# First attention of a four-layer kernel: two half-tile steps exchanged, row transposes paced, three output products one step later

## Chip, cores, metric

One core of one Trainium2 chip. The metric is the device time of one execution in microseconds (us). "Mean clock" is the mean TensorE clock that was granted over a run, 1.0 being full speed, given to three digits.

## The reference

Four residual layers on a 2048 x 576 input in bf16, in the order attention, gated layer, attention, gated layer. Cut to what matters here:

```python
def _A_ref(x, wqkv, wo):                 # 32 heads of 18, window of 8 keys at distance 2
    ...
    off = jnp.arange(W) * dil
    idx = pos[:, None] - off[None, :]
    ...
    logits = jnp.einsum('bhsd,bhswd->bhsw', q, kg) * scale
    attn = _softmax(logits, axis=-1)
    o = jnp.einsum('bhsw,bhswd->bhsd', attn, vg)
    return ... @ wo
x = A_x
x = x + _A_ref(_layernorm(x, axis=-1), A_wqkv, A_wo)
x = x + _B_ref(_layernorm(x, axis=-1), B_w_in, B_w_sp, B_b_sp, B_w_out)
...                                      # both once more
```

## The kernel before

An attention layer runs over 19 tiles of 112 query rows, each in two halves of 16 heads: 38 *half tiles*, one a step. In each step TensorE computes the scores of the next half tile (into `L_ps`), ScalarE their exponentials (`P_sb`), TensorE the products with the values of this half tile (`O_ps`), VectorE the division (`o_t`). A step also gets *fillers*: projections of later query and key columns (`pp`), value products (`pv`) and output products (`pw`).

```python
        for s in range(NST):
            if s + 1 < NST:
                L_mm(s + 1)                       # scores of the next half tile
                EXP(s + 1)
            PV(s)                                 # products with the values, division, o_t
            for f, a in table.pop(s, []):         # fillers and loads of this step
                f(*a)
```

Work that crosses partitions goes by DMA on the sync queue: projected rows are moved from `stg` into the score layout `QK` (the *moves*; GpSimd's queue takes part of them), `o_t` is transposed into `oT` (*attention transposes*), and the normalised rows of finished tiles are transposed into `xnT` (*row transposes*). Before the loop, row transposes of the layer's input do the same. The same 16 DMA engines carry the weights of the gated layer (`win2a`, `win2b`), issued on GpSimd's queue.

```python
            order = [(d, 0) for d in range(4)] + [(d, 1) for d in range(4)] + [(4, 0), (4, 1)]
            ...
            T_(12, 13, 14, 15)                    # row transposes of the layer's input
            nvw0, nvw = 4, 9
        ...
        for i in range(NS):                       # output tile i of 128 rows
            t = -(-(i + 1) * P // QT) - 1
            s = 2 * t + (6 if li == 0 and t < 10 else 5 if t < NT - 5 else 4 if t < NT - 3 else 3)
            at(s - 5, XO, i)                      # load of the residual input, for two tiles
            at(s, WO, i, 0)                       # output products, added to that input (x_new)
            at(s + 1, WO, i, 1)
            ...
            if i < NS - 1:
                at(max(s + 4, 24 + (5 * i) // 4) if li == 0 else s + 4, LN_T, i)   # row transposes
        if li == 0:
            at(0, self.load_wo, nc.sync)
            for f in reversed(self.load_win2a(nc.gpsimd)):
                at(0, f)
```

The softmax here doesn't subtract the row's maximum and nothing guards it: scores larger than these inputs give would overflow.

## Time and profile before

| what | value |
|---|---|
| time, 3 runs | 1193.89 to 1194.4 us, median 1194.13 |
| profiled run | 1192.6 us, span 1190.8 us, mean clock 0.998 |
| TensorE busy | 1180.2 us, 99% of the span |
| first attention | up to the first `pzs` product at 136.33 us |

The page gives busy times; the view of waits gives, per instruction, who ended the idle time before it; the timeline gives single instructions with start, length and, in brackets, that idle time. The lines that carry the prediction are in it. Score groups (16 score matmuls each) are good milestones, since every step has one. One group is issued before the loop; "third score group" below means the third that the loop issues.

### The profile page before, as it was taken

Reading aid. Unit: us, or ns where it says so; the run is one execution under the profiler, and the core shown is the slowest. Engines: PE = TensorE matmul, PEld = TensorE weight load, DVE = VectorE, ACT = ScalarE, POOL = GpSimd, SP = SyncE. Lnnn points to the kernel's source line nnn. Section 1 sums busy time; section 2 is a strip of 40 time slices with the busy share of each in tenths; the row PEclk is TensorE's granted clock in tenths of the full one; section 3 lists DMA queues with packets and bytes.
Section 4 is the critical chain, followed back from the end, with each engine's and each line's share of the span. In section 5 each row is a group of like instructions: output and inputs, shape, how many; then the busy total and the mean of one; then the engine's idle time right before and its main releaser. Section 6 shows DMA issues by size and latency. Waiting matters only on the chain.

```text
span 1190.8 us, 20761 instructions
## 1 busy us (share of the span) xinstructions
PE 1180.2 (99%) x8554; PEld 620.6 (52%) x8554; DVE 547.4 (46%) x1206; ACT 376.6 (32%) x593; POOL 281.5 (24%) x383
## 2 busy tenths in 40 slices
PE   8999999999999999999999999999999999999998
PEld 5567544444444444457755775444444444444677
DVE  8688587333233233245556786753233233233311
ACT  5578677210110110202156786760110110111000
POOL 4768685000000000001153877530000000000000
PEclk9999999999999999999999999999999999999999
DMA  8989992000000000049645999900000000000332
GB/s 195 200 163 199 181 224 65 23 4 9 12 12 12 12 1 11 12 139 291 169 98 117 203 227 196 202 14 9 12 12 1 12 12 12 12 1 28 125 105 73
DMA packets 178104, 101.21 MB, mean 85 GB/s; under 512 B 134336, under 2 KB 159360, under 8 KB 178009
## 3 DMA queue, kind: packets, MB, share of 16 engines
q1 hardware_dynamic: 165144, 78.13, 30.6%
q0 software_dynamic: 6512, 16.00, 5.4%
q10 hardware_dynamic: 6352, 5.75, 1.6%
q8 instruction: 67, 1.10, 0.4%
q14 instruction: 29, 0.23, 0.1%
HBM read 42.39 MB, written 16.53 MB: 49 GB/s over the span
## 4 chain that ended last, share of the span: by engine, by line
PE 94%; DMA 3%; POOL 1%; ACT 0%; issue 0%; SPq 0%; DVE 0%; ACTq 0%; DVEq 0%
PE pg L887 42%; PE pz L869 12%; PE po L941 12%; PE pz L791 11%; PE pp L402 5%; PE pw L494 3%; PE O_ps L457 3%; PE pv L379 3%; PE L_ps L437 2%; DMA oT<-o_t 2%; PE pzs L791 1%; DMA QK<-win2a 1%; POOL QK L77 1%; DMA wqk_sb<-in_A_wqkv_dram 1%; ACT P_sb L446 0%
## 5 line engine op out<-in xcount | busy, mean ns | idle before, releaser
L887 PE MATMUL pg<-Wq,Z 128*128 128x512 bf16 x2304 | 502.8, 379 | 0.0
L887 PEld LDWEIGHTS <-Z 128*128 128x128 bf16 x2304 | 225.3, 98 | 272.0
L891 DVE TENSOR_TENSOR g_tmp<-pg,ln_xn 128x512 f32<-128x512 f32 x144 | 99.6, 692 | 429.2 <-PE pg L887 429.2
L881 ACT ACTIVATE z1T<-pz 128x1024 bf16<-128x1024 f32 x72 | 73.7, 1024 | 513.8 <-PE pz L869 513.6
L77 POOL DMA_DIRECT2D wout<-in_B_w_out_dram x4 | 4.3, 1064 | 604.6 <-PE pg L887 604.6
L941 PE MATMUL po<-wout,Z 128*128 128x288 bf16 x1152 | 141.4, 286 | 0.0
L446 ACT ACTIVATE P_sb<-L_ps 128x896 bf16<-128x896 f32 (+1 forms) x152 | 126.7, 887 | 41.2 <-PE L_ps L437 40.6
L869 PE MATMUL pz<-xnT,w 128*128 128x512 bf16 (+1 forms) x640 | 136.0, 380 | 0.0
L941 PEld LDWEIGHTS <-Z 128*128 128x128 bf16 x1152 | 112.7, 98 | 28.8
L791 PEld LDWEIGHTS <-xnT 128*128 128x128 bf16 (+1 forms) x800 | 66.2, 97 | 81.0 <-issue 23.7
L791 PE MATMUL pz<-win2a,xnT 128*128 128x512 bf16 x384 | 104.8, 380 | 0.0
L892 DVE TENSOR_TENSOR Z<-g_tmp,z1T 128x512 bf16<-128x512 f32 x144 | 99.6, 692 | 9.7
L869 PEld LDWEIGHTS <-w 128*128 128x128 bf16 (+1 forms) x640 | 51.1, 97 | 80.0 <-issue 27.1
L402 PE MATMUL pp<-xnT,wqk_sb 128*128 128x512 bf16 x360 | 83.8, 382 | 0.5 <-DMA wqk_sb<-in_A_wqkv_dram 0.5
L805 ACT ACTIVATE zp<-pz 128x1024 bf16<-128x1024 f32 x64 | 65.5, 1024 | 36.6 <-PE pz L791 32.8
L951 DVE TENSOR_TENSOR x_new<-po,xo 128x288 f32<-128x288 f32 (+1 forms) x64 | 28.8, 455 | 87.6 <-PE po L941 83.5
L791 PE MATMUL pz<-win2b,xnT 128*128 128x512 bf16 (+1 forms) x256 | 65.7, 380 | 0.0
L807 DVE CUSTOM_DVE_ANT_0 Z<-zp 128x1536 bf16<-128x1536 bf16 x32 | 56.6, 1769 | 13.1 <-ACT zp L805 13.0
L77 POOL DMA_DIRECT2D QK<-stg x81 | 50.7, 631 | 36.3 <-DVE stg L371 21.0
L379 PE MATMUL pv<-wv_sb,xnT 128*128 128x288 bf16 (+1 forms) x380 | 55.8, 285 | 0.0
L242 POOL TENSOR_SCALAR ln_xn<-x_new,ln_mv,ln_rstd 128x576 bf16<-128x576 f32 x23 | 52.8, 2294 | 2.0
L402 PEld LDWEIGHTS <-wqk_sb 128*128 128x128 bf16 x360 | 33.2, 98 | 37.2 <-DMA wqk_sb<-in_A_wqkv_dram 1.0
(114 smaller groups left out, 916.9 us busy)
## 6 DMA issues: line engine op xcount, KB each, us to landing
xres<-x_new SPq DMA_DIRECT2D x48, 288.0 KB
xo<-xres SPq DMA_DIRECT2D x32, 288.0 KB
wout<-in_B_w_out_dram POOLq DMA_DIRECT2D x4, 1296.0 KB, 8.5
xo<-xres SPq DMA_DIRECT2D x8, 576.0 KB
w<-in_B_w_in_dram SPq DMA_DIRECT2D x16, 256.0 KB
QK<-stg POOLq DMA_DIRECT2D x53, 72.0 KB, 4.4
QK<-stg SPq DMA_DIRECT2D x41, 72.0 KB
xo<-in_A_x_dram SPq DMA_DIRECT2D x8, 288.0 KB
```

The lines of the kernel that those rows point to most:

```text
L77: return eng.dma_start(out=out, in_=in_)
L379: nc.tensor.matmul(pv[:nk, 0:288], lhsT=self.xnT[:, c, QT * t:QT * t + nk], rhs=wv_sb[:, c, hh * 288:(hh + 1) * 288], start=(c == 0), stop ...
L402: nc.tensor.matmul(pp[:, :], lhsT=w, rhs=self.xnT[:, c, PADL + cc * 512:PADL + (cc + 1) * 512], start=(c == 0), stop=(c == 4))
L446: nc.scalar.activation(out=P_bufs[(2 * s + jp) % 4][:nk, :, :, 0:nq], in_=Lv[:nk, :, :, 0:nq], func=ACT.Exp, scale=scale)
L791: nc.tensor.matmul(pzvs[ci][:, sub * 512:sub * 512 + w], lhsT=self.xnT[r0:r1, c, PADL + i * P:PADL + (i + 1) * P], rhs=win2(c)[r0:r1, c0 + ...
L805: nc.scalar.activation(out=zp[:, c0:c0 + cn], in_=pzvs[ci][:, 0:cn], func=ACT.Gelu_apprx_tanh, accum_out=sums[:, ci:ci + 1])
L869: nc.tensor.matmul(pz1s[q // 2][:, q % 2, :], lhsT=w1[r0:r1, c, sub * P:(sub + 1) * P], rhs=self.xnT[r0:r1, c, PADL + q * 512:PADL + (q + ...
L881: nc.scalar.activation(out=z1T[:, q2 * 512:(q2 + 2) * 512], in_=pz1s[q2 // 2][:, :, :].rearrange("p a b -> p (a b)"), func=ACT.Gelu_apprx_ ...
L887: nc.tensor.matmul(pg[:, :], lhsT=Z[:, jj, i, sub * P:(sub + 1) * P], rhs=Wq[q][:, i, :], start=(i == 0), stop=(i == NS - 1))
L891: nc.vector.tensor_tensor(out=tmp[:], in0=pg[:, :], in1=bsp[:, qs], op=ALU.add)
L892: nc.vector.tensor_tensor(out=uT(jj)[:, sub, qs], in0=tmp[:], in1=z1Ts[jj, sub][:, qs], op=ALU.mult)
L941: nc.tensor.matmul(acc[hh], lhsT=uT(j // 2)[:, j % 2, i * P:(i + 1) * P], rhs=wouts[j // NJH][:, j % NJH, hh * 288:(hh + 1) * 288], start= ...
```

## The change

It is meant for the first attention alone: let the second half tile that is computed be one whose rows arrived early (second and third step exchanged), split a weight load, start row transposes at step 19 with about one per attention tile, and put the output products of tiles 4 to 6 one step later, so that they don't wait for attention transposes. Core of the diff, cuts marked:

```diff
-        for c0, n, w0 in ((D, 512, D + 64), (0, D, 0), (D + 512, 64, D)):
+        parts = dict(k=(D, 512, D + 64), q=(0, D, 0), q0=(0, 256, 0), q1=(256, D - 256, 256), k1=(D + 512, 64, D))
+        for c0, n, w0 in (parts[k_] for k_ in names):
...
+        seq = list(range(NST))
+        if li == 0:
+            seq[1:3] = 2, 1
...
-            self.load_wqk(nc.sync)
+            self.load_wqk(nc.sync, ("k", "q0", "q1", "k1"))
...
-                    at(13 * hh, VW, t, hh, True)
+                    if hh == 1:
+                        at(0, VW, t, hh, True)
...
-            s = 2 * t + (6 if li == 0 and t < 10 else 5 if t < NT - 5 else 4 if t < NT - 3 else 3)
+            s = 2 * t + (7 if li == 0 and 5 <= t <= 7 else 6 if li == 0 and t < 10 else 5 if t < NT - 5 else 4 if t < NT - 3 else 3)
             at(s - 5, XO, i)
             at(s, WO, i, 0)
...
-                at(max(s + 4, 24 + (5 * i) // 4) if li == 0 else s + 4, LN_T, i)
+                at(s + 4 if li > 0 or i > 12 else 19 + 2 * i if i < 8 else 35 + (i - 8) // 2, LN_T, i)
         if li == 0:
+            at(1, self.fill_window_rows, QK, 1, ((4, 0),))
+            at(2, self.fill_window_rows, QK, 1, ((4, 1),))
             at(0, self.load_wo, nc.sync)
-            for f in reversed(self.load_win2a(nc.gpsimd)):
-                at(0, f)
+            w2l = self.load_win2a(nc.gpsimd)
+            for k_ in (3, 5, 4, 2, 1, 0):
+                at(0, w2l[k_])
...
         if li == 0:
             VW(nvw - 1, 0, False)
             VW(nvw - 1, 1, False)
+            VW(nvw, 0, True)
+            self.fill_window_rows(QK, 1, ((0, 0), (0, 1)))
         for s in range(NST):
             if s + 1 < NST:
-                L_mm(s + 1)
-                EXP(s + 1)
-            PV(s)
+                L_mm(seq[s + 1])
+                EXP(seq[s + 1])
+            PV(seq[s])
```

More of the change, by code (lines that the diff above doesn't have):

```diff
@@ L185, in make_ident, with fill_window_rows @@
                                 base=0, pattern=[[-1, P]], channel_multiplier=1)
-    def fill_window_rows(self, QK, half):
+    def fill_window_rows(self, QK, half, parts=((0, 0), (0, 1), (4, 0), (4, 1))):
         nc, n = self.nc, self.cfg.S // 2
@@ L193, in fill_window_rows @@
         c0 = PADL + half * n
-        for g0 in (0, 4):
-            for a in range(2):
-                nc.vector.tensor_copy(out=QK[:, a, g0:g0 + 4, c0:c0 + n].rearrange("p g (k x) -> p g k x", x=256),
-                                      in_=self.pat[:, a, None, None, PADL:PADL + 256].to_broadcast([P, 4, n // 256, 256]))
+        for g0, a in parts:
+            nc.vector.tensor_copy(out=QK[:, a, g0:g0 + 4, c0:c0 + n].rearrange("p g (k x) -> p g k x", x=256),
+                                  in_=self.pat[:, a, None, None, PADL:PADL + 256].to_broadcast([P, 4, n // 256, 256]))
     def H_tile(self, name):
@@ L284, in zero_right, with load_wqk @@
         nc.vector.memset(R["wo"][64:128, 4, :], 0.0)
-    def load_wqk(self, eng):
+    def load_wqk(self, eng, names=("k", "q", "k1")):
         R = self.right
-        for c0, n, w0 in ((D, 512, D + 64), (0, D, 0), (D + 512, 64, D)):
+        parts = dict(k=(D, 512, D + 64), q=(0, D, 0), q0=(0, 256, 0), q1=(256, D - 256, 256), k1=(D + 512, 64, D))
+        for c0, n, w0 in (parts[k_] for k_ in names):
             self.dma(R["wqk"][:, :, w0:w0 + n], self.A_wqkv[0:512, c0:c0 + n].rearrange("(c p) n -> p c n", p=P), eng=eng)
@@ L425, in layer_A @@
         NST = 2 * NT
+        seq = list(range(NST))
+        if li == 0:
+            seq[1:3] = 2, 1
+        pbi = {s: 2 * k_ for k_, s in enumerate(seq)}
         L_tiles = {}
@@ L445, in EXP @@
                 Lv = L_ps[:, :, 0:4 * QT].rearrange("p a (b c) -> p a b c", c=QT)
-                nc.scalar.activation(out=P_bufs[(2 * s + jp) % 4][:nk, :, :, 0:nq], in_=Lv[:nk, :, :, 0:nq], func=ACT.Exp,
+                nc.scalar.activation(out=P_bufs[(pbi[s] + jp) % 4][:nk, :, :, 0:nq], in_=Lv[:nk, :, :, 0:nq], func=ACT.Exp,
                                      scale=scale)
@@ L457, in PV @@
                         nc.tensor.matmul(O_ps[:, idx * (DH + 1):(idx + 1) * (DH + 1)],
-                                         lhsT=P_bufs[(2 * s + jp) % 4][:nk, jj, ftl, :],
+                                         lhsT=P_bufs[(pbi[s] + jp) % 4][:nk, jj, ftl, :],
                                          rhs=v_ext[:nk, t, 16 * hf + idx, :], start=True, stop=True)
@@ L509, in LN_XN @@
                 k_, m = divmod(i - 4, 3)
-                xn = stgs[(2 + k_) % NSTG][:].rearrange("p a b -> p (a b)")[:, 640 * m:640 * (m + 1)]
+                xn = stgs[(1 + k_) % NSTG][:].rearrange("p a b -> p (a b)")[:, 640 * m:640 * (m + 1)]
             tails[i]["xn"] = self.ln_xn(tails[i]["x"], P, mv, rstd, nmr, eng="pool", xn=xn)
@@ L650, in layer_A @@
             for hh in range(2):
-                VW(t, hh, li == 0)
+                VW(t, hh, li == 0 and t > 5)
         pieces = []
@@ L698, in layer_A @@
             if k_ == (2 if li == 0 else 0):
-                L_mm(0)
-                EXP(0)
+                L_mm(seq[0])
+                EXP(seq[0])
             PG(d, qk, cc, li > 0 or k_ < 4, q2)
-            if li == 0 and k_ == 3:
-                self.fill_window_rows(QK, 1)
         if li == 0:
```

## The prediction

> **What bounds the kernel now.** I read the page's busy times first, then TensorE's own waits, then windows of single stages, then the timeline around each gap.
>
> ```profile
> PE 1180.2 (99%) x8554; PEld 620.6 (52%) x8554; DVE 547.4 (46%) x1206; ACT 376.6 (32%) x593; POOL 281.5 (24%) x383
> ```
>
> TensorE is busy for 1180.2 of 1190.8 us, so the most that any rescheduling can win from recorded idleness is 10.6 us, 0.9%. All its waits in the run:
>
> ```profile
> PE pw L494 <- DMA oT<-o_t: 1.8, 2, 1.2
> PE L_ps L437 <- ACT P_sb L446: 1.6, 5, 0.4
> PE warm L541 <- POOL ident L184: 1.5, 1, 1.5
> PE pt L574 <- DVE ln_xn L567: 1.2, 2, 0.8
> PE L_ps L437 <- DMA QK<-win2a: 0.7, 1, 0.7
> PE pp L402 <- DMA wqk_sb<-in_A_wqkv_dram: 0.5, 1, 0.5
> ```
>
> The change touches only the first attention (up to about 136 us); the second takes the old branches, and the gated stage between them is unbroken TensorE work in the chain of waits. So a microsecond won before 136 us reaches the end whole. Busy time hides two more losses, and the windows show them (columns: length, busy time of PE, PEld, DVE, ACT, POOL with counts, granted clock, DMA share, GB/s):
>
> ```profile
> 45.00:50.00 5.00, 4.24 (x53) 2.63 (x50) 4.67 (x6) 3.75 (x6) 5.00 (x6) 1.00 1.13 220
> 50.00:55.00 5.00, 5.00 (x76) 2.41 (x74) 2.84 (x7) 2.98 (x5) 1.05 (x2) 0.66 1.07 372
> 80.00:102.60 22.60, 21.64 (x439) 15.83 (x437) 18.15 (x57) 20.18 (x26) 21.33 (x23) 1.00 0.97 197
> 123.80:136.50 12.70, 10.88 (x148) 6.62 (x144) 9.23 (x28) 5.29 (x11) 9.29 (x10) 1.00 0.97 199
> 712.20:722.90 10.70, 10.70 (x149) 6.72 (x145) 9.09 (x28) 5.35 (x11) 9.35 (x10) 1.00 1.05 211
> ```
>
> See the clock of 0.66 just after the gap at 48 us, ScalarE's 20.18 of 22.6 us in the third line, and that the last two lines are the same work (end of first and of second attention): 12.7 us against 10.7. In the timeline:
>
> ```profile
> 48.86 0.22 PE L437 MATMUL L_ps<-QK 32*128 32x112 bf16 x1 [0.69 <-DMA QK<-win2a]
> ...
> 50.90 2.29 PE L402 MATMUL pp<-xnT,wqk_sb 128*128 128x512 bf16 x5
> ...
> 54.08 1.24 PE L402 MATMUL pp<-xnT,wqk_sb 128*128 128x512 bf16 x5
> ...
> 131.51 1.39 PE L494 MATMUL pw<-wo_sb,oT 128*128 128x288 bf16 x10 [1.23 <-DMA oT<-o_t]
> ```
>
> The first score group of step 1 (heads 16 to 31) waits for the last moves of its rows; soon after it the same five projections take 2.29 us instead of 1.24; near the end an output product waits for a transpose.
>
> **What the Trainium skill says.** (1) "TensorE: Matmul & The Clock Gate", Part 1, What's actually happening: the clock is halved after a low-activity window of 4096 cycles at 1.2 GHz, 3413 ns, free-running. The trace agrees: windows of 0.1 us show the clock at 0.50 from 50.52 to 53.93 us, 3.4 us, after the thin stretch at 47.3 to 50.5. The page speaks of an idle window; here TensorE was recorded idle for only 0.7 us of it. (2) "SBUF — State Buffer", SBUF: two separate sides (the box on the DVE-blocks-DMA trap): a VectorE copy in a two-port mode keeps GpSimd from writing DMA descriptors. The trace agrees: the last of these moves is issued at 44.65 us in 1.34 us, when VectorE's four row fills (4.64 us from 44.68) begin, while the moves just before took 0.51 to 0.57. (3) "DMA: Bandwidth & Descriptors", Issuing engines are not separate DMA queues: all share the same 16 engines. The trace agrees: at 102.6 to 123.8 us, where row transposes come nearly one a step, the DMA share is 1.19.
>
> **The change part by part.** A step is scores of the next half tile (16 matmuls, 0.33 us in the chain), products of this one (0.50), and filler: a projection (five of 218 ns, 1.09), a value or output product (0.61 to 0.63).
>
> *Query weights in two loads.* The first query projection waits at 14.47 us, 0.55 us, for a load of 648 KB (576+72); its first 256 columns are 288 KB. At the 300 GB/s and more that the windows there show, 360 KB are 1.1 us, more than the wait. The projections are unbroken up to 47 us, so 0.55 us stay won.
>
> *Exchange of the second and third step.* Step 2 is heads 0 to 15 of the next tile, whose rows came earlier. Its scores don't wait; those of step 1 come a step later. I lay it out from the start of the first scores in question: scores 0.33, products 0.50, value product 0.63 (the second half of tile 9, moved here from step 13), half of the scores of step 1 to 1.62; their other half needs the second exponential of step 2, which ends at about 2.0 (0.25 plus two of 0.87); then products 0.50 and a projection 1.09: end at 3.8. Before, 47.28 to 53.19 is 5.91, with the first half of tile 9's value product in it, which now comes ahead: 5.91 against 4.43, 1.48 us won, and 0.63 of work done in advance. The rows of step 1 land before 48.82; its scores now come at about 48.9 with everything 0.55 earlier, and the move is issued up to 0.79 us sooner, since the fills start after tile 9's value product. So they should not wait. I count the clock as whole: of the 1.48, 1.05 is the slow projection; the slow 0.74 us up to 53.93 give another 0.25.
>
> *Fills and value copies.* Two fills (1.16 us each) before the loop and one in each of steps 1 and 2, behind a projection's copy. VectorE then lags: it needs about 1.5 us a step (0.26+0.46+0.69 and gaps) against TensorE's 2.1, and with four PSUM buffers I find its releases just in time (fifth products: 57.5 against 57.8). Four value copies move to ScalarE, which was idle from 34.84 to 41.78: nothing gained or lost.
>
> *Output products of tiles 4 to 6 one step on; value product taken from step 13.* In steps with one filler ScalarE bounds: steps 14 to 17 took 80.47 to 87.85 us, 1.845 each, for 1.44 of TensorE's work. Steps 13 to 24 took 24.19 us. After: steps 13 to 17 at 1.84 less some slack, 8.9; 18 to 22 with two fillers at 2.12, 10.6; step 23 1.84; step 24 2.1: 23.4. So 0.75 us of it, most of it the value product done earlier. The aim, I read, is that these products don't wait for attention transposes that the sync queue issues late (the one ready at 79.6 us was issued at 85.41).
>
> *One row transpose per attention tile, from step 19.* Before they begin at step 24 and come nearly one a step; the queue holds the attention transpose of tile 15, ready at 119.80, until 121.02 and that of tile 16, ready at 125.31, until 126.80, which lands at 131.38. Per tile the queue then needs about 1.2+1.2+0.55+0.25 = 3.2 of 4.3 us, where two row transposes made it 4.4. The second attention runs at this pace and has no such wait: 712.25 to 722.89 is 10.64 us for what took 12.69 (123.84 to 136.53). So 2.05 at most; I count 1.7, as VectorE still delivers late.
>
> Sum: 0.55+1.48+0.25+0.75+1.7 = 4.7 us. 1194.1 less 4.7 is 1189.4.
>
> **The rivals.** *A new low-clock window:* step 16 loses its only filler, 0.83 of work in 1.84 us. Over 3.4 us around it TensorE has about 2.3 of work, 67%, against about 1.9, 55%, in the window that lost its clock. For it speaks that 55% was enough; against it that 129 to 132 us, with 1.23 us idle, kept the clock at 1.00. It would cost 1 to 1.7 us: about 1190.8. If the old drop stays too, 1192. *The early row transposes delay the attention transposes:* one issued at 90.38 landed only at 99.89 (the chain of waits), which stalled VectorE by 1.59 us at 99.99, and now two or three row transposes and second-stage weights share that stretch. Against it: the second attention has this mix and no such wait. It would eat 1 to 3 us: 1190.5 to 1192.5. *The last moves of step 19's heads:* sync issues them from 80.99 to 84.78, and their scores start at 87.85; the input load that stood before them has gone behind, 0.6 us, while steps 13 to 17 shrink less than that. A wait is possible, under 1 us. *VectorE becomes the bound of steps 1 to 5* through the fills: each tenth it lags, TensorE pays; at most 0.5. *Nothing in the loop matters:* then only 0.55 comes, 1193.5; but step 1's wait and the 131.51 one lie on TensorE itself.
>
> **Range and chances.** All gains together with the full 2.05 and a little more in the exponential-bound steps give 1187.5; two rivals at once give 1192. A gain of 2% would be 23.9 us, more than twice all idleness; a loss of 2% would need a new stall in a stage that isn't touched. So faster 1%, slower 1%, same 98%.
>
> **What would show each step.** Right: no wait for query weights at 14 us and none for moved rows at 48; a clock of 1.00 in 45 to 55 us and the first projection in the loop at 1.24; steps 13 to 17 still about 1.84 apart; no output product waiting for a transpose at the end; the end of the first attention as long as the second's, 10.6 us. Wrong: a clock of 0.50 for 3.4 us around 50 or 85; VectorE or TensorE waiting for attention transposes near 95; score groups waiting for moved rows near 87.

## The result

| kernel | runs | median us | range | mean clock of the profiled run |
|---|---|---|---|---|
| before, same rounds | 6 | 1193.18 | 1191.21 to 1194.4 | 0.998 |
| changed | 6 | 1193.52 | 1191.78 to 1197.89 | 0.994 |

The ratio is 1.001, 95% interval 0.9991 to 1.003: the same time. A ratio is the mean time of one kernel's fast runs over that of the other's of the same rounds, so not quite the ratio of the medians. The prediction said 1189.4, with a range of 1187.5 to 1192: too low.

The profile of the changed kernel fell on its slowest run (1197.89 us), so what follows from it was checked on other traces. Those of e1, e3, e4, e5, e6 and e12 are of the slowest run of their kernel too, so the traces show losses more often than the timed runs have them. Its busy time, from the page:

```profile
PE 1182.9 (99%) x8554; PEld 621.0 (52%) x8554; DVE 546.5 (46%) x1202; ACT 377.5 (32%) x597; POOL 277.0 (23%) x383
```

All waits of TensorE in it:

```profile
PE pp L402 <- issue: 3.3, 1, 3.3
PE L_ps L441 <- ACT P_sb L450: 2.5, 7, 0.4
PE pt L578 <- DVE ln_xn L571: 1.9, 3, 0.8
PE warm L545 <- POOL ident L184: 1.5, 1, 1.5
```

The waits for query weights, for moved rows at 48.9 us and for a transpose near the end are gone, as predicted. A new one of 3.3 us is there. "issue" means that the wait view found no releaser; the chain of waits that leads to this projection tells more (start, length, what):

```profile
44.79 7.79 DMA xnT<-ln_xn
52.58 1.14 issue
53.72 2.29 PE pp L402 x5
```

A row transpose of the layer's input, the third of the last four, took 7.79 us to land. The 1.14 us after it are the fourth: the semaphore on which it counts is complete at 53.63 us, 7.46 us after its issue at 46.17, and the projection's first weight load starts at 53.69. The windows (columns as in the prediction) show what came with it, and the end of the first attention in the last line:

```profile
45.00:50.00 5.00, 4.65 (x76) 3.21 (x75) 2.51 (x3) 3.77 (x7) 3.49 (x5) 1.00 1.20 166
50.00:55.00 5.00, 1.71 (x20) 0.82 (x19) 1.83 (x6) 1.14 (x2) 0.88 (x2) 0.75 1.01 271
55.00:60.00 5.00, 5.00 (x73) 2.24 (x72) 3.14 (x6) 2.05 (x3) 0.00 (x0) 0.57 0.49 172
82.30:105.96 23.66, 22.54 (x429) 15.74 (x428) 17.93 (x53) 18.66 (x24) 19.99 (x24) 0.86 0.90 195
130.10:140.80 10.70, 10.70 (x149) 6.72 (x145) 8.91 (x28) 5.20 (x11) 9.05 (x10) 1.00 0.98 196
```

The stretch from 45 to 50 us is fuller than before (4.65 against 4.24 us busy), but the clock falls twice: to a mean of 0.57 in 55 to 60 us, and to 0.86 in the long stretch. In the clock records both are 6.83 us at 0.50, from 52.5 and from 90.04 us. The end of the first attention takes 10.7 us, TensorE without a gap, as the second attention did. The timeline around the first trouble:

```profile
47.38 0.40 PE L441 MATMUL L_ps<-QK 32*128 32x112 bf16 x16
...
49.57 0.37 PE L441 MATMUL L_ps<-QK 32*128 32x112 bf16 x8 [0.35 <-ACT P_sb L450]
49.87 0.56 PE L461 MATMUL O_ps<-v_ext,P_sb 128*128 128x19 bf16 x16
53.72 2.29 PE L402 MATMUL pp<-xnT,wqk_sb 128*128 128x512 bf16 x5 [3.29 <-issue]
```

The exchanged scores start without a wait at 47.38, those of step 1 wait only for the exponentials: the exchange works as intended. Right behind it the first projection of the loop stands 3.29 us, and runs at half speed. So TensorE reaches the end of the first attention (first `pzs` product) at 140.61 us, 4.28 later than in the profile of before.

### The profile page after: what moved, and what is told of

It reads as the page before. It is cut to its first block, busy times and chain, and to the rows that moved or that the text cites. A ratio compares the mean times of both kernels' runs of the same rounds, so it can differ in the third digit from the quotient of the medians.

```text
span 1196.1 us, 20760 instructions
## 1 busy us (share of the span) xinstructions
PE 1182.9 (99%) x8554; PEld 621.0 (52%) x8554; DVE 546.5 (46%) x1202; ACT 377.5 (32%) x597; POOL 277.0 (23%) x383
## 4 chain that ended last, share of the span: by engine, by line
PE 96%; DMA 1%; DVE 1%; ACT 1%; issue 1%; POOL 0%; SPq 0%; ACTq 0%; DVEq 0%
PE pg L895 42%; PE pz L877 12%; PE po L949 12%; PE pz L799 11%; PE pp L402 7%; PE pv L379 3%; PE pw L498 3%; PE O_ps L461 3%; PE L_ps L441 2%; PE pzs L799 1%; DMA xnT<-ln_xn 1%; DMA oT<-o_t 1%; ACT P_sb L450 1%; DVE ln_st L558 0%; PE pt L479 0%
## 5 line engine op out<-in xcount | busy, mean ns | idle before, releaser
L959 DVE TENSOR_TENSOR x_new<-po,xo 128x288 f32<-128x288 f32 (+1 forms) x64 | 28.8, 456 | 87.9 <-PE po L949 83.7
```

## Experiments

All outputs are right. The times of "before" in a batch are those of the same chip and rounds. Unless an edit is marked otherwise it is against the changed kernel.

### Is the new wait in every run, and what causes it?

**e1_again**: the changed kernel, unaltered.

> The changed kernel again, unaltered, for a second profile and more times. Theory A (the changed kernel's own schedule lost the gain: the last row transpose before the loop lands late, and step 16 without filler loses the clock): the first projection of the loop waits 2 us or more for a transposed row tile again, a clock of 0.50 shows for one or two windows of 3.4 us after step 16 or after that wait, and the end of the first attention takes 10.6 to 10.7 us as in the profile after; the time is within 2 us of before. Theory B (the profiled run of 1197.89 us was an accident): no such wait, and the time is 3 to 5 us under before.

Median 1193.83 (1192.32 to 1195.75) against 1191.06, ratio 1.001 (0.9991 to 1.003). Its trace has the wait again, with its releaser named:

```profile
52.87 1.45 PE L402 MATMUL pp<-xnT,wqk_sb 128*128 128x512 bf16 x5 [2.66 <-DMA xnT<-ln_xn]
```

The clock is at 0.50 for 3.41 us from 53.77 and for 6.83 us from 87.9. Two of its six runs had a mean clock of 1.0, so the low clock is not in every run.

**e3_weights_later**: the second stage's first weight loads at step 3 instead of step 0.

```diff
-                at(0, w2l[k_])
+                at(3, w2l[k_])
```

> The changed kernel with the six loads of the second stage's weights issued at step 3 and not at step 0. Theory A1 (these loads, which the exchange brought forward, crowd the last row transpose): the transpose lands at 48 to 50 us, the first projection of the loop doesn't wait, and the time is 2.5 to 4 us under the changed kernel's. Rival A2 (the transposes are slow by themselves, or held by the semaphore eight DMAs back): the wait of 2 to 3 us stays and so does the time.

1199.13 (1197.48 to 1200.61) against 1191.06, ratio 1.0051 (1.0031 to 1.0072): slower. The wait for the row transpose is gone (the fourth lands 2.7 us after its issue), and so is the low clock near 50 us; but in its place, from the view of waits and from the chain:

```profile
PE pw L498 <- DMA oT<-o_t: 5.5, 1, 5.5
```

```profile
59.58 11.86 DMA oT<-o_t
```

The six loads were issued from 58.01 to 61.31 us, around that attention transpose, and a low clock follows, 6.83 us from 68.49. So the transfers that are late lie beside the loads at either place: row transposes at step 0, an attention transpose at step 3.

**e5_loads_behind_moves**: the same six loads at step 0 in another order: those whose place in `win2a` still serves as `stg` buffer go first, so that all six wait for it (in the trace, until the third row transpose, which reads it, has landed at 48.30 us).

```diff
-            for k_ in (3, 5, 4, 2, 1, 0):
+            for k_ in (2, 1, 0, 3, 5, 4):
```

> The changed kernel with one line altered: the six weight loads of the second stage in the order 2, 1, 0, 3, 5, 4. Piece 2 overwrites rows that are still being moved out, so it and all behind it are issued only when those moves have landed (about 47 us in the first experiment, where the loads began at 44.6). Theory A1 (early loads crowd the last row transpose): the last row transpose lands by 50.5 us, the first projection's wait of 2.7 to 3.3 us shrinks to under 0.8, and the time falls by 2 us or more against the changed kernel where no low-clock window differs. Rival A2 (transposes are slow by themselves): the wait stays.

1191.84 (1190.26 to 1194.99) against 1191.08, ratio 1.0006 (0.9992 to 1.0021). The issue of these loads in the timeline, kernel before first:

```profile
44.65 1.34 POOL L77 DMA_DIRECT2D QK<-win2a  x1 [0.57 <-DMA QK<-win2a]
45.99 5.07 POOL L77 DMA_DIRECT2D win2a<-in_B_w_in_dram  x6
```

The changed kernel:

```profile
42.55 2.09 POOL L77 DMA_DIRECT2D QK<-win2a  x4 [0.17 <-issue]
44.63 1.68 POOL L77 DMA_DIRECT2D win2a<-in_B_w_in_dram  x3
```

This run:

```profile
48.40 3.88 POOL L77 DMA_DIRECT2D win2a<-in_B_w_in_dram  x6 [4.11 <-DMA xnT<-ln_xn]
```

In this trace of before, the last move was issued while VectorE's fills ran, and took 1.34 us; the loads began at 45.99 us. The change put these fills later, so the moves went out faster, as I had predicted, and three weight loads began at 44.63 us, in the middle of the four row transposes (issued from 42.14 to 47.43 us). Begun at 48.40, they do no harm: no wait for a row transpose, no low clock near 50 us, and the third score group starts at 51.22 us (55.95 and 54.25 in the two traces of the changed kernel). The packets fit. The transposes move as packets of 256 bytes, the weights as packets of 4608. In the kernel before, about 1660 packets of 256 bytes were carried from 46 to 49 us; in the changed kernel 240 from 48 to 51 us, where the weight packets take 0.74 to 1.06 us each instead of 0.2 to 0.3. Why they take longer there isn't shown; VectorE's last two fills run at that time (47.86 to 50.22 us).

Five traces have the changed order of loads and all four transposes. In each the first projection starts within 0.15 us of the fourth transpose's landing, also where the view puts the wait to VectorE (e2, e13); and its wait is long where the loads begin early: 2.66, 3.29, 1.78, 0.57 and 0.31 us for loads from 44.46, 44.63, 44.73, 44.94 and 45.12 us (e1, the changed kernel, e17, e2, e13). Nor is the old order safe. In e4 and e8 below, which keep the old fills and loads, the last move went out just before the fills, in 0.51 us, the loads began at 44.32 and 44.44 us, and the first projection waits for a row transpose as well, 1.30 us (e4) and 0.39 us (e8):

```profile
51.30 1.24 PE L402 MATMUL pp<-xnT,wqk_sb 128*128 128x512 bf16 x5 [1.30 <-DMA xnT<-ln_xn]
```

So loads that begin early go with that wait in either kernel; with the change they begin early more often (five of five traces at 45.12 us or before, against two of six: before, e4, e8, e10, e14, e18).

**e6_last_row_tile_on_pe**: the last of the four row tiles is transposed by TensorE instead.

```diff
-            T_(12, 13, 14, 15)
+            T_(12, 13, 14)
...
+        if li == 0:
+            T_pe(15)
```

> The changed kernel with the row transpose of tile 15 done by TensorE (5 matmuls, about 0.3 us, and one copy on ScalarE) and not by a DMA: it takes away what the first projection waits for. Theory A: no wait there, the low-clock window at 50 to 57 us goes, the loop's third score group starts at about 51.6 us (54.2 and 56.0 in the two profiles of the changed kernel); time 2 to 3 us under the changed kernel's. The window at 88 us stays. If the gain shows at 56 us but not in the total, a wait for attention transposes at steps 18 to 26 has taken it.

1192.08 (1191.03 to 1193.03) against 1191.08, ratio 1.0005 (0.9992 to 1.0019). The wait is gone too, the third score group starts at 51.70 us. So two independent edits take the wait away; but that brings the time only to that of before, and the intervals of both overlap that of the changed kernel (0.9991 to 1.003): the gain is seen in the traces, not in the times.

### Low clock in the thin steps, and step (c)

**e2_products_back**: the output products of tiles 4 to 6 at their old steps.

```diff
-            s = 2 * t + (7 if li == 0 and 5 <= t <= 7 else 6 if li == 0 and t < 10 else ...)
+            s = 2 * t + (6 if li == 0 and t < 10 else ...)
```

> The changed kernel with the output products of tiles 4 to 6 back at their old steps, so that step 16 has a filler again. Theory A: no low clock near 90 us; 1.5 to 3 us faster than the changed kernel in those of its runs that lose that window, about equal in the others; a wait of the early row tile stays. Rival (the shift was needed against late attention transposes): output products at steps 16 to 20 wait for attention transposes, up to 2 us, and the time is no better.

1194.27 (1193.42 to 1195.95) against 1191.06, ratio 1.0016 (0.9997 to 1.0035). No low clock at 80 to 92 us in its trace, but 2.4 us of waits for attention transposes, the longest 1.7, and low clock at 50.52 and 108.54 us. The time is that of the changed kernel. Its trace has new waits in place of the low clock near 90 us; that these just make up for it is not shown.

**e7_and_filler_in_step16**: as e6, with five unread matmuls of 288 columns in step 16, the one that lost its only filler.

```diff
+        def FILLER():
+            pf_ = self.PT_tile([P, 512], f32, "idle_fill")
+            for _ in range(5):
+                nc.tensor.matmul(pf_[:, 0:288], lhsT=self.ident[:], rhs=wv_sb[:, 0, 0:288], start=True, stop=True)
...
+        for s_ in (16,) if li == 0 else ():
+            at(s_, FILLER)
```

> As e6, and step 16 gets five matmuls of 288 columns whose result nobody reads (0.62 us, in time in which TensorE waits for ScalarE anyway). Theory (low activity of step 16 loses the clock): no low-clock window at 85 to 97 us in the profile, and the median clock of the runs rises to 0.999 or more; another 1.5 to 3 us under e6. Rival (the attention transposes bound this stretch, and the slow clock only fills a wait that would stand there anyway): the window goes, but an output product at steps 18 to 26 then waits 1.5 to 4 us for an attention transpose and the time stays.

1192.16 (1190.27 to 1196.43) against 1191.08, ratio 1.001 (0.9992 to 1.0029). Its trace has full clock from start to end. The steps 13 to 24 nevertheless take 26.21 us (24.19 before), since VectorE waits for the residual input of an output product:

```profile
84.88 0.42 SPq L77 DMA_DIRECT2D xo<-in_A_x_dram  x1
```

```profile
89.65 0.46 DVE L501 TENSOR_TENSOR x_new<-pw,xo 128x288 f32<-128x288 f32 x1 [3.83 <-DMA xo<-in_A_x_dram]
```

That load moved with its product, to behind four moves in the sync queue: issued at 84.88 us, landed at 89.65; in the kernel before it was issued at 80.38. TensorE lost 1.5 us to it.

**e9_input_load_back**: as e7, the load at its old step.

```diff
-            at(s - 5, XO, i)
+            at(s - 6 if li == 0 and 5 <= t <= 7 else s - 5, XO, i)
```

> The kernel of the run with the last row tile on TensorE and the filler, with one more edit: the residual input loads for the output products of tiles 4 to 6 are issued at their old steps, while the products stay one step later. Theory (the load that was moved with its product lands too late): there the load was issued at 84.88 us and landed at 89.65, VectorE waited 3.8 us for it and TensorE 1.5. Issued one step earlier it stands before the moves, near 80.4 us as in the kernel before, so that wait disappears, and the time from the 14th to the 26th score group falls from 26.06 us to between 23.3 and 24.5. First pzs product then at 132 to 133.2 us (134.48 there), the whole 1.3 to 2.5 us less than that kernel's clean 1190.3, near 1188.3 (median of before about 1191). Rival (second-stage weight loads starve whatever is in flight there): the load is issued earlier but lands as late, or the wait passes to attention transposes, and the stretch stays at 26 us. Second rival: with that wait gone the steps run into the next attention transpose at about 100 us, as in the run with the row transposes alone, and 1 to 3 us come back there.

1191.09 (1190.5 to 1192.59) against 1191.41, ratio 0.9998 (0.9983 to 1.0013). The load is issued at 79.84 us, VectorE's wait is gone, and the first `pzs` product starts at 133.49 us (134.48 in e7). From the 14th to the 26th score group, the one before the loop counted, it took 24.93 us, a little over my 24.5, and the median missed my 1188.3 by 2.8 us.

**e11_load_back_no_filler**: the same without the filler.

> As the run with the input load back, but without the unread filler products in step 16. If the low clock near 86 us came from the step that lost its filler alone, one window of 3.41 us at a halved clock stays at 80 to 92 us and costs up to 1.7 us against the run with filler (1190 against 1188.3). If it came from the wait for the input load and the thin step together, the clock stays at 1.00 there and both kernels have the same time.

1191.77 (1190.37 to 1195.21) against 1191.41, ratio 1.0003 (0.9987 to 1.0019). The same stretch of both, first e11, then e9:

```profile
76.67:88.00 11.33, 10.21 (x216) 7.12 (x216) 8.23 (x25) 9.19 (x12) 10.88 (x14) 0.82 0.92 163
```

```profile
76.57:88.00 11.43, 10.56 (x228) 7.75 (x227) 8.14 (x25) 10.11 (x12) 10.98 (x14) 1.00 0.97 161
```

Without filler the clock drops (0.82, third number from the right; in the clock records 6.83 us at 0.50 from 83.96 us), with it it stays. The first `pzs` product comes at 134.62 instead of 133.49 us, although the filler's 0.61 us of work are not done: the window costs about 1.7 us against e9, and 2.4 against e16, which has fewer waits there. Over all traces: the eight of changed kernels with the thin step (the changed kernel, e1, e3, e5, e6, e11, e13, e17) all have low clock that begins between 80 and 93 us. In seven of them it begins 0.5 to 2.5 us after step 16; in e13 it begins 6.9 us after it, behind a wait of 1.32 us for VectorE, so that the thin step is an unlikely cause (e5 has another before step 16, at 80.87). Of the five with the filler, e7, e9 and e16 have none, e12 and e15 have it, after a wait of more than 1 us there. Of the six that are the kernel before or one part of the change on it, e10 and e18 have it. The timed runs are a check with more cases, though they don't tell where the clock was low: 7 of the 47 of kernels with the thin step have a mean clock of 1.0, 15 of the 28 with the filler, 34 of 71 of the kernel before; in the pair e11 and e9 it is 1 and 3 of 6. Part of this is other windows, as the one near 53 us. So the thin step is not the only cause and doesn't act in every run, but with it a low clock is much more frequent.

### Other parts by themselves

**e4_row_transposes_only**: the kernel before with the new row-transpose steps.

```diff
-                at(max(s + 4, 24 + (5 * i) // 4) if li == 0 else s + 4, LN_T, i)
+                at(s + 4 if li > 0 or i > 12 else 19 + 2 * i if i < 8 else 35 + (i - 8) // 2, LN_T, i)
```

> The kernel before with one part of the change alone: one row transpose per attention tile. By my prediction the end of the first attention shrinks from 12.7 to 10.7 us and the time falls by 1.7 to 2.1 us, with nothing else changed up to 98 us (the low-clock window at 50 us stays). Rival (early row transposes delay the attention transposes at 90 to 100 us): VectorE waits for them for 2 us or more there and half the gain or more is lost.

1191.72 (1189.61 to 1195.22) against 1191.06, ratio 0.9995 (0.9973 to 1.0017). The trace is that of its slowest run, 1195.22 us: an output product waits 3.3 us for an attention transpose before 107.63 us, and low clock follows from 107.89. A loss of that size doesn't fit its runs at 1189.61 and 1190.03. That the early row transposes delayed it is likely, as they are the edit, but one trace doesn't show it. The wait for a row transpose before the loop's first projection (above) is in this trace too.

**e8_exchange_only**: the kernel before with `seq` alone.

> The kernel before with one part of the change alone: the second and third step exchanged. By my prediction the wait of 0.69 us for moved rows and 1.4 us of the gap at 47 to 49 us go. Theory A1 (here the weight loads start no earlier than in the kernel before, about 46 us): the last row transpose lands at about 50 us, the first projection waits less than 0.8 us, so 0.5 to 1.2 us faster than before. Rival: the first projection waits for the row transpose for 2 us or more here too, because the wait of step 1 had merely hidden it, and nothing is won.

1191.78 (1191.05 to 1192.32) against 1191.08, ratio 1.0004 (0.999 to 1.0017). The second-step wait is gone, the third score group starts at 51.55 us; near the end an output product waits 2.0 us for its transpose and the clock drops from 130.26 us. Exchange and row transposes may need each other; but one trace is little for that, and together they bring no more.

**e10_query_split_only**: the kernel before with the query weights in two loads.

> The kernel before with the query weights in two loads and nothing else. My step (a) says 0.55 us are won: no wait for these weights at 14 us, first scores 0.5 to 0.6 us earlier, everything up to the gated stage 0.55 us earlier unless a later wait eats it (the row moves at 48.86 us then wait longer, since their transfers are set by VectorE and GpSimd: rival, gain 0.2 or less). It also tells whether the 0.75 us that the end of the program lost in the changed kernel comes with this part: 3.05 us from the last product to the end if not, about 3.75 if so.

1192.71 (1191.08 to 1196.26) against 1191.41, ratio 1.0011 (0.9994 to 1.0028). First scores at 40.53 us, but they come at 40.89 and 40.80 in the two later traces of before, which have no wait for these weights. So 0.3 to 0.4 us, not 0.55; and in six traces of changed kernels the time of these scores varies by 0.3 us (40.37 to 40.65). And from the last product to the end this kernel takes 3.7 us, where before takes 3.05.

### The end of the program

Each row is from one trace. The transfers of the sync queue, and ScalarE's last output with them, count on eight semaphores in turn; in the last column but one is the place, in the order in which the closing block waits for them, of the one on which the last output counts:

```
kernel               last output lands   its place   last product to end
before, e14               2.1 us           8th           3.05 us
changed                   2.1              2nd           3.80
e2                        2.1              2nd           3.42
e10 (query split)         2.4              2nd           3.7
e9                        2.1              1st           3.88
e12, e13                  2.1              1st, 2nd      3.88, 3.84
e16, e17                  2.1              8th           3.06, 3.05
```

**e12_last_piece_on_act_queue** (e9 with one small weight load issued by ScalarE's queue) and **e13_changed_end_restored** (the changed kernel with two):

```diff
-            self.load_wqk(nc.sync, ("k", "q0", "q1", "k1"))
+            self.load_wqk(nc.sync, ("k", "q0", "q1"))
+            self.load_wqk(nc.scalar, ("k1",))          # e13; e12: only its 64-row piece
```

> The kernel of the input load back (last row tile on TensorE, filler, input load at its old step), with one small weight load (64 rows of the last 64 key columns) issued by ScalarE's queue instead of the sync queue. In the trace the sync queue's transfers count on eight semaphores in turn, and the closing block waits for these one after the other, about 0.07 us each. In the kernel before, the last output lands on the eighth of them (2.13 us after the last product) and the end is at 3.05; the query weights in two loads shift the turn, the last output lands on the first or second, six or seven waits follow it, and the end is at 3.7 to 3.9. Theory: with one transfer less on the sync queue it lands on the eighth again, and last product to end is 3.0 to 3.1 us: 0.7 us won, median near 1190.4 where before has about 1191.3, the fastest runs near 1189.8. Rival (the longer end comes from fetching instructions at another place of the stream): the end stays at 3.4 us or more.

> The changed kernel with both loads of the last 64 key columns issued by ScalarE's queue, so that the sync queue has as many transfers as before. Theory: last product to end 3.0 to 3.1 us against 3.75; all else, the wait for the last row transpose near 53 us too, as in the changed kernel: 0.7 us less than it, about 1193.0, still above before. Rival as in the run before this one: the end stays at 3.4 or more.

1191.42 (1190.23 to 1194.08) and 1192.32 (1190.62 to 1195.6) against 1191.32, ratios 1.0001 (0.9988 to 1.0013) and 1.0011 (0.9997 to 1.0025). Inconclusive for the end: the last output still landed on the first or second semaphore, so the edit didn't change what it was to change. The traces gave something else: e12, with the load in front of the moves again, waits for moved rows,

```profile
PE L_ps L441 <- DMA QK<-stg: 1.5, 2, 1.1
```

and e13, with the load behind them, has VectorE waiting 3.2 us for the load. So each of two transfers can be late behind the other; but not in every run, for e9 and e16 have the load in front as well and don't wait for moved rows.

**e16_last_piece_on_gpsimd_queue** (e9) and **e17_changed_end_restored_again** (the changed kernel), with the small loads on GpSimd's queue instead:

```diff
+            self.load_wqk(nc.gpsimd, ("k1",))          # e17, after the set-up; e16: only its 64-row piece
```

> The runs that moved small loads to ScalarE's queue left the last output on the first or second semaphore of the turn, so both hardware queues share the turn and those runs didn't test the theory. Here the input-load-back kernel has the 64-row piece of the last key columns on GpSimd's queue, which counts on other semaphores. Theory: the last output lands on the eighth semaphore as in the kernel before, one wait follows it, and last product to end is 3.0 to 3.1 us instead of 3.9: 0.8 us won, a median of about 1190.3 to 1190.8 where before has 1191.3, and runs with full clock near 1189.8. This is also my candidate to beat both kernels, at most by 0.1%. Rival (another place in the instruction stream makes the end longer): it stays at 3.4 or more.

> The changed kernel with both loads of the last 64 key columns on GpSimd's queue, so that the hardware queues have as many transfers as before. Theory: last product to end 3.0 to 3.1 us against 3.75, the rest as in the changed kernel (a wait for the last row transpose near 53 us, one or two low-clock windows): median 1192.5 to 1193.2, runs with full clock near 1191.7 against 1192.4. Rival: the end stays at 3.4 or more.

1191.51 (1189.34 to 1193.27) and 1192.98 (1190.48 to 1195.56) against 1192.02, ratios 1.0001 (0.9983 to 1.0019) and 1.0011 (0.9992 to 1.003). The last output counts on the eighth semaphore, and the end is back at 3.05 us in both: the extra two transfers of the split query load had shifted the turn, and six or seven waits of about 0.07 us, one of them 0.4 in the changed kernel, e9, e12 and e13 (in e2 none, and its end is 3.42), stood behind the last output. Why one is longer is open. This explains 0.75 us of the 1197.89 us run, in e2 0.37. In the rest, e17 behaves as the changed kernel: a row transpose is waited for 1.78 us, and there are low-clock windows at 52.73 and 86.86 us.

The profiled run of e16 (1189.34 us, span 1187.6) is the cleanest of all; TensorE's waits in it:

```profile
PE L_ps L441 <- ACT P_sb L450: 2.4, 7, 0.4
PE pz L888 <- issue: 1.6, 10, 0.2
PE warm L551 <- POOL ident L184: 1.5, 1, 1.5
PE pt L585 <- DVE ln_xn L578: 0.8, 2, 0.5
```

No wait for a transfer is left (the second line stands at places where matmul records are missing: the trace has 8467 matmuls for 8564 weight loads). It is my candidate to beat both kernels, and it doesn't beat the one before: its other five runs took 1190.39 to 1193.27 us.

**e15_second_weights_every_third_step**: e12 with the later weight loads spread.

```diff
-            at(PG_END + 2 + 2 * k_, win2b_piece, k_)
+            at(PG_END + 2 + (3 if li == 0 else 2) * k_, win2b_piece, k_)
```

> As the first of these four, and the six later weight loads of the second stage begin every third step (16, 19 to 31) instead of every second (16, 18 to 26). Theory (these loads slow the attention transposes): VectorE's wait for oT transposes between 85 and 100 us (1.4 us, which TensorE paid with 0.58) goes away, and up to 0.6 us are won against that kernel; rival: the loads meet the row transposes later, at 103 to 118 us, and delay transposes there, so that nothing is won or up to 2 us lost.

1193.52 (1191.37 to 1194.4) against 1191.32, ratio 1.0015 (1.0003 to 1.0027). Slower by more than its reason can tell: 1.8 us of waits for moved rows near 86 us and 6.83 us of low clock from 87.18, before the spread loads matter. It settles nothing about these loads.

### Were the losses that I counted in every run of before?

**e14_before_again** and **e18_before_third_trace**: the kernel before, unaltered.

> The kernel before, unaltered, for a second trace. Theory: the low clock at 50.5 us that I counted as a loss of every run is in some runs only (24 of 33 runs of it had a mean clock of at least 0.999). If this trace has full clock, the first pzs product begins near 134.6 us instead of 136.33, the third score group near 51.9 instead of 53.13, and the output product near the end still waits 1 us or more for its transpose. Rival: it's there again at 50 us, and clean runs differ in something else. Ratio 1.000.

> The kernel before once more, for a third trace. Of its 55 timed runs beside my experiments 27 had a mean clock of 1.0 and a mean time of 1190.4 us, 2 us less than the run whose profile I predicted from. Theory (the losses that my steps (b) and (d) counted are not in every run): if this run has full clock, the first pzs product begins at 133 to 134.2 us (136.33 in the profile that I read, 135.02 in the second trace), the projection in step 1 takes 1.24 us, and the output product near the end waits 0.7 us or less for its transpose; the run's time is then 1189.2 to 1191. If it has a low-clock window at 50 us again, it is 1191 to 1193.5. Rival: with full clock the first attention ends at 135 to 136.3 us all the same, and the 2 us are elsewhere.

1191.76 (1189.91 to 1193.08) against 1191.32, ratio 1.0003 (0.999 to 1.0016); and 1191.94 (1190.42 to 1199.72) against 1192.25, ratio 1.0015 (0.9978 to 1.0052). The windows that showed the low clock, e14 then e18:

```profile
50.00:55.00 5.00, 5.00 (x75) 2.41 (x74) 2.81 (x7) 2.90 (x5) 0.74 (x2) 0.66 1.05 366
```

```profile
50.00:55.00 5.00, 4.89 (x89) 2.77 (x88) 3.31 (x9) 4.32 (x6) 0.84 (x3) 1.00 1.05 365
```

In e18 the clock is full there: 89 matmuls instead of 75 in the same 5 us. Its timeline:

```profile
48.15 0.22 PE L437 MATMUL L_ps<-QK 32*128 32x112 bf16 x1 [0.92 <-DMA QK<-win2a]
...
50.17 1.24 PE L402 MATMUL pp<-xnT,wqk_sb 128*128 128x512 bf16 x4
51.34 0.70 PE L437 MATMUL L_ps<-QK 32*128 32x112 bf16 x16
...
130.32 1.39 PE L494 MATMUL pw<-wo_sb,oT 128*128 128x288 bf16 x10 [1.10 <-DVE o_t L464]
```

The wait for moved rows is there in all three traces (0.69, 1.0 and 0.92 us). But the slow projections are not, and without them the kernel before reaches its third score group at 51.34 us, as early as the best changed one. e18 has its low clock at 84.16 us instead, so neither run is a trace of before with full clock throughout; such a trace I don't have.

Timed runs by their mean clock (of before, the 62 beside the experiments):

```
kernel                      runs   mean us    at clock 1.0: runs   mean us
before                       62    1191.8            29            1190.5
changed (with e1)            12    1194.0             2            1192.4
e9                            6    1191.4             3            1191.4
e16                           6    1191.4             5            1191.0
```

With the nine runs of e14 and e18, before has 71 runs, mean 1191.9, of which 34 at clock 1.0 take 1190.6. Chips differ, so the rounds matter: in those of e9 and e16 before took 1190.2 and 1189.9 us at clock 1.0 (five runs each). At full clock both candidates are thus about 1 us behind it.

## Why the prediction was wrong

Two steps failed. The exchange, 1.48 + 0.25 of the 4.7 us, was counted from a loss that not every run of before has; against a run without it, it wins nothing (-0.12 us). And the sum holds nothing for what the change itself costs: a row transpose that lands late (up to 3.29 us), a clock window in the thin step (1.7 to 2.4), and the end of the program (0.75).

**The base.** I took 4.7 us off 1194.1, the median of three runs. Of 62 later runs of the same kernel 29 had full mean clock and took 1190.5 us on average, and the mean of all is 1191.8. The three lay high (only 6 of the 62 took 1193.89 us or more), and the profiled run (1192.6) had low clock at 50 us. The losses were real, but some were of that run and not of the kernel. My own sentence "a microsecond won before 136 us reaches the end whole" holds; that each loss there is in every run was never said and silently used. The base is not what made the number too low: 4.7 us off 1191.8 would be 1187.1, further off still.

**Step by step**, the prediction's figure first; then what e16, which has all parts of the change and no accident, wins in its trace against the profile I read and against the two later traces of before. The times of both kernels stand in brackets; the five filler matmuls of e16 are taken off with 0.61 us, what they lengthen step 16 (2.05 us in e9, 1.44 in e11). The first row still holds 0.28 us for the five transposing matmuls of e6 (38.20 to 38.48 us in e16), which the change as given doesn't have: without them it reads 0.85, 0.43 and 0.34.

| step | predicted | against the first profile | against e14 | against e18 |
|---|---|---|---|---|
| query weights: start to first score group | 0.55 | 0.57 (41.31, 40.74) | 0.15 (40.89) | 0.06 (40.80) |
| exchange: group before the loop to its third | 1.48 + 0.25 | 1.16 (11.82, 10.66) | 1.84 (12.50, low clock) | -0.12 (10.54) |
| steps 13 to 24 | 0.75 | 0.32 (24.19, 23.87) | 0.09 (23.96) | 1.82 (25.69, low clock) |
| end of first attention | 1.7, at most 2.05 | 2.05 (12.69, 10.64) | 0.89 (11.53) | 1.05 (11.69) |

*Query weights and end.* The working was right for the run that I read, even to the 2.05 that I cut to 1.7. But the wait for query weights is in one of three traces of before, and near the end, where the same output product waits in all three (1.23, 0.72 and 1.10 us), the first profile has a second wait for a transpose of 0.6 us. As a difference between kernels these two steps are about 0.4 and 1.0.

*Exchange.* 1.05 of its 1.48 and the 0.25 were the low clock, which "I count as whole". e18 has full clock there, and the exchange wins nothing against it: the value product done ahead costs 0.60 us (6.58 us from the group before the loop to the loop's first, against 5.98), and from the loop's first to its third e16 takes 4.08 us for my 3.8, since the scores wait 0.35 us for exponentials. Two more traces with full clock there agree: the old order takes 10.16 us in e10, the exchange alone 10.60 in e8. That is the step of the prediction that failed most.

*Steps 13 to 24.* ScalarE's bound was right: for six steps, 13 to 18, I had 8.9 and 2.12, 11.02 us; e16 took 11.63 with the filler, and e13, without it and at full clock there, 11.21. The other six took 12.85 us for my 12.42 (four of 2.12, 1.84 and 2.1); steps 23 and 24 alone took 4.28 for my 3.94, as their scores wait 0.42 us for exponentials. So 0.3 instead of 0.75, and 0.1 against the quicker e14.

Against a run of before with no low clock I therefore estimate 0.4 - 0.1 + 0.1 + 1.0, about 1.4 us, from the entries without it.

**What took even this 1.4 us**, none of it in the sum:

1. A row transpose of the layer's input lands late (3.29, 2.66, 1.78, 0.57 and 0.31 us of TensorE's time in the traces of the changed kernel, e1, e17, e2 and e13). The prediction saw that the move would be "issued up to 0.79 us sooner", and stopped there; what stood behind the moves on GpSimd's queue, weight loads, came 1.36 us sooner than in that profile as well. e5 and e6 show it; e4 and e8 show that the old order can meet it too.
2. Low clock in the thin step. It was the first rival, with a cost of "1 to 1.7 us", and it came in seven of the eight traces with that step. I had named it and given it no place in the predicted time.
3. The residual input's load. The prediction used its later place ("has gone behind, 0.6 us") as a help to the moves and did not ask who waits for the load. e7 and e9 show it, where nothing earlier hides it. e12 and e15 have the load in front and pay at the moves, the third rival; e9 and e16 have it there and do not.
4. The end: 0.75 us through the turn of the semaphores, shown by e16 and e17. No step or rival of mine had it.

The second rival (early row transposes delay attention transposes) is seen in the one trace of e4, 3.3 us; its median shows no loss, so how often it happens is open. VectorE's lag in steps 1 to 5 was not found: in e16 those steps have no wait for it. The third point that the prediction takes from the skill is shown less well than it says: a DMA share of 1.19 shows busy engines, not that queues share them; e5 speaks to that.

With these removed one by one (e5, e6, e9, e16) the changed kernel comes back to the time of before, not below it (ratios 1.0006, 1.0005, 0.9998 and 1.0001, each within noise of the 1.001 of the changed kernel); of what is left of its gain 0.61 us go into the filler and 0.28 into the transposing matmuls. e16's runs at clock 1.0 range from 1189.34 to 1192.17 us; what its slower ones lose at full clock isn't known, since only one run has a trace. One place that varies is the second attention, whose eighth step took 3.87 to 4.73 us in traces of kernels with the same code there, with an output product waiting for its transpose: 3.87 or 3.88 us in all six traces of before and of one part on it, 4.07 to 4.73 in six of the seven with the row tile on TensorE (e6, e7, e9, e11, e12, e16; e15 has 3.88), and 4.03 to 4.26 in three of the seven other changed ones. So the remedies may cost something there; why isn't known. Whether the change as given is slower than before stays open by the intervals; both comparisons gave 1.001, and 1.0011 in e13 and e17, which differ from it in one small load.

## What to carry to other kernels

Before a loss in a profile is counted as a gain, see whether it's in a second trace: at 99% busy, what is left to win is about as large as what differs between runs. When a change makes one queue faster, list what stands behind it in that queue and what it will meet; when work moves, list the loads that move with it. And a step that loses its only filler on a busy matrix engine can cost a clock window, 1.7 to 2.4 us here.

## What the Trainium skill lacked or had wrong

- "TensorE: Matmul & The Clock Gate", Part 1, speaks of an idle window before the clock is halved. Here it halved after 3.41 us in which TensorE was recorded idle for 0.7 us (before), and after steps 16 and 17 with no wait over 0.44 us (changed). Up to the program's end the windows of low clock were 3.41 or 6.83 us long in every trace, once or twice the page's 3413 ns. The same page's section "A second HAM failure mode: psum-queue depth-cycling" tells of micro-idles that do this, nearer to what the runs show; it gives no threshold, nor do they.
- "DMA: Bandwidth & Descriptors", Queues, rings and completion order: the engines take turns between queues by packets. The runs fit this, though no view shows the turns, and give the size of what follows, which the page lacks: beside loads in packets of 4608 bytes, transposes in packets of 256 landed up to 7.79 us after issue, in e3 11.86, and moving the loads by 3.8 us took the first wait away (e5).
- "SBUF — State Buffer", the box on the DVE-blocks-DMA trap, agreed (a move issued in 1.34 us under VectorE's fills, 0.51 to 0.57 without). What it doesn't say: the slowed queue kept later loads out of the way in that trace, and loads that began earlier cost 0.3 to 3.3 us.
- No page that I found tells in what order the end of the program waits for the semaphores of transfers: with the last output on the eighth of eight the last product to the end took 3.05 us, on the first or second 3.4 to 3.9.
